# Forgetting attention and a SwiGLU block on one core: q and k read as neighbouring rows, weights spread over later pairs

## The chip, the cores and the metric

The kernel runs on one core of one Trainium2 chip. The metric is the device time of one execution in microseconds. Matrix work runs on TensorE (PE); VectorE (DVE), ScalarE (ACT) and GpSimd (POOL) do the rest, and SyncE (SP) issues most of the transfers between device memory and the on-chip buffer. PE writes its results to PSUM.

## The reference

There are 8 batches of 8 heads, 576 tokens and a head width of 64. The attention result, 4608 tokens by 512, goes through a gated feed-forward block (FFN) with 1536 inner columns.

```python
scores = scale * np.matmul(q, k.transpose(0, 1, 3, 2))
cum = np.cumsum(np.log(np.clip(f, 0.0001, 1.0)), axis=-1)
decay = cum[:, :, :, None] - cum[:, :, None, :]
scores = np.where(causal, -1000000000.0, scores + decay)   # causal: above the diagonal
attn = softmax(scores)                                     # with 1e-09 in the divisor
x = np.matmul(attn, v)                                     # as tokens x (heads * 64)
g = x @ w_gate
out = (g * (1.0 / (1.0 + np.exp(-g))) * (x @ w_val)) @ w_out
```

## The kernel before, in words

**Pairs.** Two heads are worked on together as a pair; there are 32 pairs, four to a batch. For pair `p` the steps are these:

- `load_qk` loads `qf` and `kf` in float32, each with two DMAs (one a head). Partition `r` of 96 holds rows `r`, `r + 96`, and so on, six of them, so each row is a run of 64 numbers, 256 bytes, in memory.
- `cast_qk` makes them `kb` and `qb` in bfloat16. From pair 4 on this runs on POOL alone; before that the planner may also choose ACT or DVE.
- `transposes` (L409) turns `kb` and `qb` on PE into a PSUM tile `tt`, six matmuls of 96 columns each. There is one `tt` buffer. `kt` is copied out by ACT (L415), and the two halves of `qz`, one a head, by DVE or ACT (L420).
- `scores` runs nine blocks of 64 query rows in the order 8, 4, 5, 6, 7, 0, 1, 2, 3. PE writes `sp` (L491, with the mask added by L494); one DVE instruction adds the decay `cb` and takes the minimum, the "reduce" of this text (L507); ACT takes the exponential and its sum (L525). After blocks 8 and 4 to 7, and again after 0 to 3, DVE takes reciprocals `rl` (L534, L535), and POOL writes the normalised blocks into `pk` (L548).
- `turned` transposes `pk` into `pT`: for the first four pairs by PE and copies (L583, L588), later by a DMA transpose from SP (L570). `weighted` multiplies by `v` (L616) and copies into `xT` (L626).

`load_v` brings a batch's `v` in five pieces, `load_cum` the decay of a pair, broadcast over 64 partitions.

**FFN.** There are nine tiles of 512 tokens. A tile needs `xT` of all four pairs of the batches that it touches. For each of 12 column blocks `gate` runs four matmuls each for `gp` and `vp` (L658), then a tanh on ACT (L664) and two DVE instructions (`u` L668, `hh` L674). `project` runs 12 matmuls for each of four output blocks (L705), a copy (L712 or L714) and a store (L718). `gp`, `vp`, `op` and the PSUM tile of `turned` share four PSUM buffers (`gv`).

**Weights.** `weights` loads `wg`, `wv` and `wo` in eleven pieces through POOL's DMA queue (L737, L742), converting to bfloat16 on the way. Each piece waits for a "tick", one particular exponential.

**Order.** Nothing here is in program order. Each step is given to `Planner.add` with the engines it may run on, a due time (`key`), a modelled length and, for DMAs, a modelled time on the transfer queue (`moves`). `Planner.order` plays these forward: each free engine takes the ready step with the lowest key for which buffers are free. The instructions are then emitted in that order on every engine. A change of a modelled length or a key can so move instructions on all five engines. `base(p)` is the due time of a pair, `unit_key(n)` that of an FFN unit:

```python
SLOT0, SLOT = 9.5, 12.0
UNIT = SLOT / 4
def unit_key(n):
    return base(NPB) + 3.0 * SLOT0 + UNIT * n
```

Of the kernel before, what the change touches and what calls it, by code (L numbers as in the profile page):

```python
# [20 lines left out]
class Planner:  # L21
# [4 lines left out]

    LAG = {"PE": 0.25, "DVE": 0.2, "ACT": 0.25, "POOL": 0.12, "SP": 0.0}
    LAND = 2.2

    def __init__(self, counts):  # L30
        self.counts = counts
# [13 lines left out]
    def order(self):  # L45
# [35 lines left out]
        while len(started) < len(steps):  # L81
            moved = True
            while moved:
                moved = False
                for e in self.LAG:
                    if free[e] > t + 1e-9:
                        continue
                    kept, pick = [], None
                    while ready[e]:
                        x = heapq.heappop(ready[e])  # L90
                        n = x[1]
                        if n in started:
                            continue
                        ok = True
                        for b in steps[n][4]:
                            c = b[0]
                            if c in self.counts and len(opened[c]) >= self.counts[c] \
                                    and open_users[opened[c][-self.counts[c]]]:
                                ok = False
                        if ok:  # L100
                            pick = n
                            break
                        kept.append(x)
                    for x in kept:
                        heapq.heappush(ready[e], x)
                    if pick is None:
                        continue
                    n = pick
                    engines, key, fn, needs, opens, moves = steps[n]
                    started.add(n)  # L110
                    for b in opens:
                        if b[0] in self.counts:
                            opened[b[0]].append(b)
                    end = t + engines[e]
                    free[e] = end
                    if moves:
                        queue = max(queue, end) + moves
                        end = queue + self.LAND
                    self.ends[n] = end
                    heapq.heappush(events, (end + self.LAG[e], 0, n))  # L120
                    heapq.heappush(events, (free[e], 1, n))
                    out.append((t, n, e))
                    moved = True
            if not events:
                assert len(started) == len(steps), "the steps wait for each other"
                break
            t = max(t, events[0][0])
            while events and events[0][0] <= t + 1e-9:
# [24 lines left out]
def kernel(  # L153
# [47 lines left out]
            return 0, 1  # L201
        return (g == 1) + c * w, sum(i // 2 >= c for i in GROUPS[g])

    KR, KC = 96, 6
    NRING = 5 * MT
    EARLY = NPB

    consts = ctx.enter_context(tc.tile_pool(name="consts", bufs=1))
    keep = ctx.enter_context(tc.tile_pool(name="keep", bufs=1))
# [58 lines left out]
        return 10.0 + (SLOT0 * p if p <= NPB else SLOT0 * NPB + SLOT * (p - NPB))  # L268

    def unit_key(n):  # L270
        return base(NPB) + 3.0 * SLOT0 + UNIT * n


    def gates():
# [48 lines left out]
        for p in range(2):  # L323
            key = base(0) + 3 if p else -5
            a = add("ACT" if p else "SP", -7 if p else -9, 1.2, load(p), opens=[("t", "fb", p)],
                    moves=0.8)
            a = add("DVE", key, 0.4, clip(("fb", p)), [a], uses=[("t", "fb", p)])
            w = add("ACT", key, 0.6, ln(("fb", p)), [a, w], uses=[("t", "fb", p)])
            ids["cb", p] = add("DVE", key, 1.3, scan(p), [w, o], opens=[("cb", p)],
# [8 lines left out]
    def load_cum(p):  # L338
        def fn():
# [4 lines left out]
                    in_=cum_dram[2 * p + h:2 * p + h + 1, :].to_broadcast((64, S)),  # L344
                )
            st["cb", p] = cb
        ids["cb", p] = add("SP", base(p) - 9, 1.1, fn, [ids["cum"]], opens=[("cb", p)], moves=0.8)

    def zeros():
        def z(n):  # L350
# [15 lines left out]
    def load_qk(p):  # L366
        b, hp = divmod(p, NPB)
        for name, src, off in (("kf", k, -0.2), ("qf", q, 0.0)):
            eng = "ACT" if p == 0 and name == "qf" else "SP"

            def fn(name=name, src=src, eng=eng):
                st[name, p] = ldf.tile([KR, KC, 2, D], F32, name=name)
                for h in range(2):
                    (nc.scalar if eng == "ACT" else nc.sync).dma_start(  # L374
                        out=st[name, p][:, :, h, :],
                        in_=src[b, 2 * hp + h].rearrange("(c r) d -> r c d", r=KR),
                    )

            after = [ids["exp", p - 3, 4]] if p > 2 else [ids["kb", 0]] if p == 2 else []
            ids[name, p] = add(eng, base(p) - 20 + off if p else -8, 1.2, fn, after,  # L380
                               opens=[(name, p)], moves=1.3)

    def cast_qk(p):
        def cq(eng):
            st["qb", p] = att.tile([KR, KC, P], BF16, name="qb")
            qf = st["qf", p].rearrange("r c h d -> r c (h d)")
            if eng is nc.scalar:
                eng.mul(st["qb", p], qf, -scale)
            else:
                eng.tensor_scalar(st["qb", p], qf, -scale, 1.0, op0=ALU.mult, op1=ALU.mult)  # L390

        def ck(eng):
            st["kb", p] = att.tile([KR, KC, P], BF16, name="kb")
            copy_by(nc, eng)(st["kb", p], st["kf", p].rearrange("r c h d -> r c (h d)"))  # L394

        engines = {"POOL": 0.79, "ACT": 0.72, "DVE": 0.88} if p < EARLY else {"POOL": 0.79}
        for name, fn, off in (("kb", ck, -9.2), ("qb", cq, -9)):
# [5 lines left out]
    def transposes(p):  # L403

        def tr(name):
            def fn():
                st["tt", name] = psum([P, S], BF16, "tt", "tt")
                for c in range(KC):
                    nc.tensor.transpose(st["tt", name][:, KR * c:KR * c + KR], st[name, p][:, c, :],  # L409
                                        ident[0:KR, 0:KR])  # L410
            return fn

        def ek(eng):
            st["kt", p] = att.tile([P, S], BF16, name="kt")
            copy_by(nc, eng)(st["kt", p], st["tt", "kb"])  # L415

        def eq(h):
            def fn(eng):
                r = slice(64 * h, 64 * h + 64)
                copy_by(nc, eng)(qzs[p % 2][r, :, h, :],  # L420
                                 st["tt", "qb"][r, :].rearrange("p (i r) -> p i r", r=QB))
            return fn
        a = add("PE", base(p) - 5, 0.3, tr("kb"), [ids["kb", p]], opens=[("tt", p, 0)],
                uses=[("kb", p)])
        ids["kt", p] = [add("ACT", base(p) - 5, 0.54, lambda: ek(nc.scalar), [a], opens=[("kt", p)],
                            uses=[("tt", p, 0)])]
        a = add("PE", base(p) - 4, 0.3, tr("qb"), [ids["qb", p]], opens=[("tt", p, 1)],
                uses=[("qb", p)])
        before = [ids["s", p - 2, i] for i in range(NB)] if p >= 2 else [ids["z", p]]
        ids["qz", p] = [add({"DVE": 0.38, "ACT": 0.53}, base(p) - 4, 0, eq(h), [a] + before,  # L430
                            uses=[("tt", p, 1)]) for h in range(2)]

    def load_v(b):
# [4 lines left out]
        for c in range(5):  # L438
# [17 lines left out]
            buf = ("hh", "v") if b == 0 else ("vf", b, c)  # L456
            opens = [buf] if b or c == 0 else []
            after = [ids["exp", NPB * (b - 1) + min(c, 3), 4] if b else ids["qf", 1]]
            a = add("SP", key, 0.5, load, after, opens=opens, uses=[] if opens else [buf], moves=1.1)
            ids["v", b].append(add({"POOL": 0.58, "ACT": 0.5, "DVE": 0.6} if b == 0 else {"POOL": 0.58},  # L460
                                   key + 10 if b else base(0) + 3 + 0.1 * c, 0,
                                   cast if b == 0 else lambda cast=cast: cast(nc.gpsimd),
# [5 lines left out]
    def scores(p):  # L468
# [8 lines left out]
        for i in ORDER:  # L477
# [6 lines left out]
            for n, (a, z) in enumerate(parts):  # L484
                last = z == L

                def s(i=i, a=a, z=z, last=last):
                    qz = qzs[p % 2].rearrange("p i h r -> p i (h r)")
                    sp = psum([P, 512], F32, "sp", "sp")
                    st["sp", p, i, a] = sp  # L490
                    nc.tensor.matmul(sp[:, :z - a], qz[:, i, :], st["kt", p][:, a:z],  # L491
                                     start=True, stop=not last)
                    if last:
                        nc.tensor.matmul(sp[:, z - a - QB:z - a], ident, mask,  # L494
# [66 lines left out]
    def turned(p, g, n_slots, ns, key):  # L561
# [7 lines left out]
            new()  # L569
            nc.sync.dma_start_transpose(out=st["pT", p, g], in_=src.rearrange("p s k -> p (s k)"))  # L570
        if p >= EARLY:
            m = add("SP", key, 1.35, by_dma, ns, opens=[(f"pT{g}", p)], moves=0.144 * n_slots)
            ids["turn", p, g] = [m]
            ids["pT", p, g] = [m]
            return
# [157 lines left out]
    def weights():  # L733
# [12 lines left out]
        for n in range(4):  # L746
            ids["w", n] = []
            for wt, src in ((wg, moe_w_gate), (wv, moe_w_val)):
                ids["w", n].append(add("POOL", base(0) + 6 + 5 * m, 0.96, piece(wt, src, n),
                                       [ids["tick", m]], moves=2.6))  # L750
                m += 1
        ids["wo"] = []
        for fc in range(0, KF, 4):
            ids["wo"].append(add("POOL", base(0) + 6 + 5 * m, 0.96, piece_out(fc), [ids["tick", m]],
                                 moves=3.4))
            m += 1


# [5 lines left out]
    for b in range(B):  # L764
        for p in range(NPB * b, NPB * b + NPB):
# [4 lines left out]
                load_cum(p)  # L770
            transposes(p)
            scores(p)
            if p == NPB - 1:

                order = [ids["exp", p_, i] for p_ in range(NPB) for i in ORDER]
                for n in range(11):
                    ids["tick", n] = order[2 + 3 * n]
                weights()

            while True:  # L780
                t = ids.get("tiles", 0)
                if t >= NMT or (t + 1) * MT > (b + (p % NPB == NPB - 1)) * S:
                    break
                n = 0 if t == 0 else KF + (t - 1) * (KF + NS)
                for fc in range(KF):
                    gate(t, fc, n)
                    n += 1
                    if t and fc % 3 == 2:
                        project(t - 1, fc // 3, n)
                        n += 1  # L790
                ids["tiles"] = t + 1
        if b + 1 < B:
            load_v(b + 1)
    n = KF + (NMT - 1) * (KF + NS)
    for s_ in range(NS):
        project(NMT - 1, s_, n)
# [34 lines left out]
```

## Time and profile before

| | |
|---|---|
| median of 3 runs | 457.19 us (456.84 to 457.54) |
| the profiled execution's own time | 458.71 us |
| its span, first to last instruction | 456.9 us |
| first FFN matmul starts at | 67.87 us |
| PE busy | 409.9 us (90%), granted clock 0.970 in the mean |
| DVE / ACT / POOL busy | 340.2 / 300.2 / 245.7 us |
| DMA queue q1 (SP) | 213,712 packets, 69.71 MB, 68.4% of 16 engines' span |
| DMA queue q0 (weights) | 5,808 packets, 4.72 MB, 6.8% |

Busy time is what an engine spent in instructions; waits are not in it. The page also cuts the span into 40 slices of 11.4 us and gives each engine's busy tenths in them. A timeline line reads: start in us, length in us, engine, source line, operation, tile written from tile read, size; an idle time before the instruction, with what ended it, stands in brackets. A share of the DMA queues is the time that packets took, summed over queues, so it can pass 100% of 16 engines where packets wait.

### The profile page before, as it was taken

The page shows a single profiled execution, that of the slowest core. Times are in us where ns is not written, and L with a number is a line of the kernel's source. Part 1 is how long each engine was busy: PE and PEld are TensorE (multiplying, and loading weights), DVE is VectorE, ACT ScalarE, POOL GpSimd, SP SyncE. Part 2 cuts the span into 40 slices and gives each one's busy share as a digit, 9 for nine tenths or more (in the row PEclk, how much of TensorE's full clock was granted, in tenths as well). Part 3 has the DMA queues.
Part 4 walks back from the last instruction along what each step waited for, and adds up shares of the span by engine and source line. Part 5 has one row for each costly group of instructions (what it writes and reads, how often), then busy time and mean ns, then how long its engine had stood idle before and what let it go on. Part 6 is the DMA issues. An engine that isn't in the chain of part 4 may idle for free.

```text
span 456.9 us, 9377 instructions
## 1 busy us (share of the span) xinstructions
PE 409.9 (90%) x2788; PEld 211.3 (46%) x2836; DVE 340.2 (74%) x1069; ACT 300.2 (66%) x838; POOL 245.7 (54%) x443
## 2 busy tenths in 40 slices
PE   1557777988989999999999999999999999999996
PEld 0345453444444454554555455445555444444442
DVE  5756578788777989889889888888888864565542
ACT  3875678488776887787887779778777743213210
POOL 5574878378882785666666666666654440000000
PEclk9997589899989999999999999999999999999999
DMA  7999999959997799898799989899983540100103
GB/s 168 181 185 247 213 215 180 220 137 214 227 207 181 133 214 222 179 223 217 190 217 199 207 192 221 192 223 214 196 203 96 99 117 24 46 25 23 46 25 115
DMA packets 220996, 75.77 MB, mean 166 GB/s; under 512 B 206480, under 2 KB 212112, under 8 KB 220944
## 3 DMA queue, kind: packets, MB, share of 16 engines
q1 hardware_dynamic: 213712, 69.71, 68.4%
q0 software_dynamic: 5808, 4.72, 6.8%
q10 hardware_dynamic: 1424, 0.74, 0.7%
q8 instruction: 22, 0.36, 0.3%
q14 instruction: 30, 0.25, 0.2%
HBM read 47.33 MB, written 9.58 MB: 125 GB/s over the span
## 4 chain that ended last, share of the span: by engine, by line
PE 65%; DVE 2%; issue 1%; DMA 1%; ACT 1%; SPq 1%; POOL 0%; DVEq 0%
PE op L705 18%; PE vp L658 17%; PE gp L658 17%; PE sp L491 6%; PE xo L616 5%; PE tt L409 2%; PE sp L494 1%; DMA pT<-pk 1%; DVE t L507 1%; DVE ot L714 0%; DVE rl L534 0%; ACT ev L525 0%; SPq L374 0%; DVE hh L674 0%; POOL pk L548 0%
## 5 line engine op out<-in xcount | busy, mean ns | idle before, releaser
L548 POOL TENSOR_SCALAR pk<-ev,rl 128x512 bf16<-128x512 f32 (+3 forms) x320 | 165.0, 535 | 95.9 <-DVE tm L507 32.7
L525 ACT ACTIVATE ev<-t,tm 128x64 f32<-128x64 f32 (+8 forms) x288 | 159.9, 557 | 40.6 <-DVE tm L507 29.2
L507 DVE CUSTOM_DVE_ANT_0 t<-sp,cb 128x512 f32<-128x512 f32 (+7 forms) x288 | 132.0, 477 | 17.5 <-PE sp L494 9.0
L658 PE MATMUL vp<-xT,wv 128*128 128x512 bf16 x413 | 121.8, 382 | 1.9 <-issue 1.0
L658 PE MATMUL gp<-xT,wg 128*128 128x512 bf16 x418 | 119.1, 385 | 3.8 <-DVE u L668 3.2
L705 PE MATMUL op<-wo,hh 128*128 128x512 bf16 x418 | 119.9, 379 | 0.9 <-DVE u L668 0.2
L491 PE MATMUL sp<-kt,qz 128*128 128x64 bf16 (+1 forms) x319 | 89.7, 298 | 18.5 <-DVE tm L507 15.6
L664 ACT ACTIVATE th<-gp 128x512 f32<-128x512 f32 x108 | 62.5, 588 | 58.2 <-PE gp L658 57.0
L668 DVE SCALAR_TENSOR_TENSOR u<-th,gp 128x512 f32<-128x512 f32 x108 | 73.2, 684 | 33.4 <-ACT th L664 33.1
L674 DVE TENSOR_TENSOR hh<-u,vp 128x512 bf16<-128x512 f32 x108 | 73.3, 682 | 15.0 <-PE vp L658 12.8
L705 PEld LDWEIGHTS <-hh 128*128 128x128 bf16 x432 | 39.2, 98 | 42.9 <-issue 0.8
L494 PE MATMUL sp<-mask,ident 128*128 128x64 bf16 x288 | 55.7, 198 | 0.0
L525 ACT ACTIVATION_READ_ACCUMULATOR ev<-t,tm 128x1 f32 x288 | 54.6, 190 | 0.0
L658 PEld LDWEIGHTS <-wg 128*128 128x128 bf16 x432 | 36.4, 99 | 37.0 <-issue 6.2
L658 PEld LDWEIGHTS <-wv 128*128 128x128 bf16 x432 | 36.1, 98 | 34.1 <-issue 1.4
L491 PEld LDWEIGHTS <-qz 128*128 128x128 bf16 x320 | 32.0, 101 | 39.0 <-issue 5.5
L494 PEld LDWEIGHTS <-ident 128*128 128x128 bf16 x288 | 28.5, 99 | 36.7 <-issue 17.5
L616 PE MATMUL xo<-pT,vt 128*64 128x320 bf16 (+4 forms) x448 | 35.5, 274 | 3.6 <-ACT vt L454 1.9
L616 PEld LDWEIGHTS <-vt 128*64 128x64 bf16 x448 | 20.4, 110 | 26.4 <-issue 17.0
L626 ACT CAST xT<-xo 128x320 bf16<-128x320 f32 x64 | 25.0, 390 | 11.0 <-PE xo L616 10.6
L394 POOL CAST kb<-kf 96x768 bf16<-96x768 f32 x30 | 27.0, 900 | 7.2 <-DMA kf<-in_k_dram 7.2
L454 POOL CAST vt<-vf 128x512 bf16<-128x512 f32 (+1 forms) x35 | 21.4, 610 | 17.4 <-DMA vf<-in_v_dram 12.1
(50 smaller groups left out, 283.0 us busy)
## 6 DMA issues: line engine op xcount, KB each, us to landing
kf<-in_k_dram SPq DMA_DIRECT2D x64, 144.0 KB, 3.3
out_dram<-ot SPq DMA_DIRECT2D x36, 256.0 KB, 2.6
qf<-in_q_dram SPq DMA_DIRECT2D x62, 144.0 KB, 3.5
cb<-cum_f SPq DMA_DIRECT2D x60, 144.0 KB, 3.4
vf<-in_v_dram SPq DMA_DIRECT2D x28, 256.0 KB, 3.6
wg<-in_moe_w_gate_dram POOLq DMA_DIRECT2D x4, 384.0 KB, 7.3
wv<-in_moe_w_val_dram POOLq DMA_DIRECT2D x4, 384.0 KB, 9.2
wo<-in_moe_w_out_dram POOLq DMA_DIRECT2D x3, 512.0 KB, 10.2
```

The source lines that it names most:

```text
L394: copy_by(nc, eng)(st["kb", p], st["kf", p].rearrange("r c h d -> r c (h d)"))
L491: nc.tensor.matmul(sp[:, :z - a], qz[:, i, :], st["kt", p][:, a:z], start=True, stop=not last)
L494: nc.tensor.matmul(sp[:, z - a - QB:z - a], ident, mask, start=False, stop=True)
L507: nc.vector.tensor_tensor_reduce(out=st["t", p, i][:, a:z], in0=st["sp", p, i, a][:, :z - a], in1=st["cb", p][:, a:z], scale=1.0, scalar=init,
L525: nc.scalar.activation(evs[i][:, :L], st["t", p, i][:, :L], AF.Exp, bias=tm[:, i:i + 1], scale=-1.0, accum_out=ls[:, i:i + 1])
L548: nc.gpsimd.tensor_scalar(pks[p % 2][:, s0:s0 + w * (m - 1) + 1:w, :], evs[i][:, P * c:P * (c + m)].rearrange("p (c k) -> p c k", k=P), st ...
L616: nc.tensor.matmul(xo[64 * h:64 * h + 64, 0:n * QB], vt[:, c, 2 * hp + h, :], pT[:, s0:s0 + n, h, :], start=(c == 0), stop=(c == nch - 1))
L658: nc.tensor.matmul(st[name, t, fc], w_[:, ko, fc * P:(fc + 1) * P], xT[:, ko, x0:x0 + MT], start=(ko == 0), stop=(ko == KD - 1))
L664: nc.scalar.activation(st["th", t, fc], st["gp", t, fc], AF.Tanh, scale=0.5)
L668: nc.vector.scalar_tensor_tensor(st["u", t, fc], st["th", t, fc], 1.0, st["gp", t, fc], op0=ALU.add, op1=ALU.mult)
L674: nc.vector.tensor_mul(st["hh", t][:, fc, :], st["u", t, fc], st["vp", t, fc])
L705: nc.tensor.matmul(st["op", t, s_], st["hh", t][:, fc, s_ * P:(s_ + 1) * P], wo[:, fc, :], start=(fc == 0), stop=(fc == KF - 1))
```

## The change

Six things are edited.

1. `q` and `k` are read so that a partition holds neighbouring rows: six for `k` (96 partitions, runs of 1536 bytes), eight for `q` (72 partitions, runs of 2048 bytes). Both heads come in one DMA. The tile is laid out head first; the cast puts chunks first again.
2. `k` is transposed in six matmuls of 96 columns as before, `q` in eight of 72. A transposed chunk now holds every sixth or eighth token, and the copies out of PSUM put them in order: they read PSUM with a step of 96 or 72 elements.
3. The weights' ticks go from exponentials 2, 5, ... 32 of the first four pairs to 9, 13, ... 49, which is pairs 1 to 5.
4. Pair 0's `k` and `q` get an earlier key than the loads of `f`, so that they lead the queues of SP and ACT.
5. The planner gets a limit: a step that opens a buffer and moves data is held back while the modelled transfer queue is more than 5 us long. FFN units are due one `SLOT0` (9.5) later. Some modelled lengths and `moves` change.
6. The FFN tiles and the weights are added to the plan after a batch's pairs, from batch 1 on, instead of after each pair. Their dependencies are the same.

```diff
+    CHUNKS = {"k": (96, 6), "q": (72, 8)}
+    WFIRST, WSTEP = 9, 4
 # Planner
+    AHEAD = 5.0
+                        if steps[n][5] and queue - t > self.AHEAD:
+                            heapq.heappush(events, (queue - self.AHEAD, 2, n))
+                            ok = False
 # unit_key
-        return base(NPB) + 3.0 * SLOT0 + UNIT * n
+        return base(NPB) + 4.0 * SLOT0 + UNIT * n
 # load_qk
-                st[name, p] = ldf.tile([KR, KC, 2, D], F32, name=name)
-                for h in range(2):
-                    (nc.scalar if eng == "ACT" else nc.sync).dma_start(
-                        out=st[name, p][:, :, h, :],
-                        in_=src[b, 2 * hp + h].rearrange("(c r) d -> r c d", r=KR),
-                    )
+                nr, nch = CHUNKS[name[0]]
+                st[name, p] = ldf.tile([nr, 2, nch, D], F32, name=name)
+                (nc.scalar if eng == "ACT" else nc.sync).dma_start(
+                    out=st[name, p].rearrange("r h c d -> r h (c d)"),
+                    in_=src[b, 2 * hp:2 * hp + 2].rearrange("h (r c) d -> r h (c d)", c=nch),
+                )
...
-            ids[name, p] = add(eng, base(p) - 20 + off if p else -8, 1.2, fn, after,
-                               opens=[(name, p)], moves=1.3)
+            ids[name, p] = add(eng, base(p) - 20 + off if p else -10, 0.6, fn, after,
+                               opens=[(name, p)], moves=1.0)
 # cast_qk (kb likewise)
-            st["qb", p] = att.tile([KR, KC, P], BF16, name="qb")
-            qf = st["qf", p].rearrange("r c h d -> r c (h d)")
+            st["qb", p] = att.tile([*CHUNKS["q"], 2, D], BF16, name="qb")
+            qf = st["qf", p].rearrange("r h c d -> r c h d")
 # transposes
-                for c in range(KC):
-                    nc.tensor.transpose(st["tt", name][:, KR * c:KR * c + KR], st[name, p][:, c, :],
-                                        ident[0:KR, 0:KR])
+                nr, nch = CHUNKS[name[0]]
+                for c in range(nch):
+                    nc.tensor.transpose(st["tt", name][:, nr * c:nr * c + nr],
+                                        st[name, p][:, c, :, :].rearrange("r h d -> r (h d)"),
+                                        ident[0:nr, 0:nr])
...
-            copy_by(nc, eng)(st["kt", p], st["tt", "kb"])
+            nr, nch = CHUNKS["k"]
+            copy_by(nc, eng)(st["kt", p].rearrange("p (r c) -> p r c", c=nch),
+                             st["tt", "kb"].rearrange("p (c r) -> p r c", c=nch))
...
-                copy_by(nc, eng)(qzs[p % 2][r, :, h, :],
-                                 st["tt", "qb"][r, :].rearrange("p (i r) -> p i r", r=QB))
+                nr, nch = CHUNKS["q"]
+                copy_by(nc, eng)(
+                    qzs[p % 2][r, :, h, :].rearrange("p i (r c) -> p i r c", c=nch),
+                    st["tt", "qb"][r, :].rearrange("p (c i r) -> p i r c", c=nch, i=NB))
...
-        ids["qz", p] = [add({"DVE": 0.38, "ACT": 0.53}, base(p) - 4, 0, eq(h), [a] + before,
+        ids["qz", p] = [add({"DVE": 0.6, "ACT": 0.55}, base(p) - 4, 0, eq(h), [a] + before,
 # the ticks of the weights
-                order = [ids["exp", p_, i] for p_ in range(NPB) for i in ORDER]
+            order = [ids["exp", p, i] for p in range(2 * NPB) for i in ORDER]
...
-                    ids["tick", n] = order[2 + 3 * n]
+                ids["tick", n] = order[WFIRST + WSTEP * n]
```

More of the change, by code (lines that the diff above doesn't have):

```diff
@@ L202, in slots_of @@
         return (g == 1) + c * w, sum(i // 2 >= c for i in GROUPS[g])
-    KR, KC = 96, 6
+    CHUNKS = {"k": (96, 6), "q": (72, 8)}
     NRING = 5 * MT
     EARLY = NPB
+    WFIRST, WSTEP = 9, 4
     consts = ctx.enter_context(tc.tile_pool(name="consts", bufs=1))
@@ L325, in gates @@
             a = add("ACT" if p else "SP", -7 if p else -9, 1.2, load(p), opens=[("t", "fb", p)],
-                    moves=0.8)
+                    moves=1.0)
             a = add("DVE", key, 0.4, clip(("fb", p)), [a], uses=[("t", "fb", p)])
@@ L346, in fn @@
             st["cb", p] = cb
-        ids["cb", p] = add("SP", base(p) - 9, 1.1, fn, [ids["cum"]], opens=[("cb", p)], moves=0.8)
+        ids["cb", p] = add("SP", base(p) - 9, 1.1, fn, [ids["cum"]], opens=[("cb", p)], moves=1.0)
     def zeros():
@@ L392, in ck @@
         def ck(eng):
-            st["kb", p] = att.tile([KR, KC, P], BF16, name="kb")
-            copy_by(nc, eng)(st["kb", p], st["kf", p].rearrange("r c h d -> r c (h d)"))
+            st["kb", p] = att.tile([*CHUNKS["k"], 2, D], BF16, name="kb")
+            copy_by(nc, eng)(st["kb", p], st["kf", p].rearrange("r h c d -> r c h d"))
         engines = {"POOL": 0.79, "ACT": 0.72, "DVE": 0.88} if p < EARLY else {"POOL": 0.79}
@@ L424, in transposes @@
                 uses=[("kb", p)])
-        ids["kt", p] = [add("ACT", base(p) - 5, 0.54, lambda: ek(nc.scalar), [a], opens=[("kt", p)],
+        ids["kt", p] = [add("ACT", base(p) - 5, 0.56, lambda: ek(nc.scalar), [a], opens=[("kt", p)],
                             uses=[("tt", p, 0)])]
@@ L458, in load_v @@
             after = [ids["exp", NPB * (b - 1) + min(c, 3), 4] if b else ids["qf", 1]]
-            a = add("SP", key, 0.5, load, after, opens=opens, uses=[] if opens else [buf], moves=1.1)
+            a = add("SP", key, 0.5, load, after, opens=opens, uses=[] if opens else [buf], moves=1.45)
             ids["v", b].append(add({"POOL": 0.58, "ACT": 0.5, "DVE": 0.6} if b == 0 else {"POOL": 0.58},
@@ L490, in s @@
                     st["sp", p, i, a] = sp
-                    nc.tensor.matmul(sp[:, :z - a], qz[:, i, :], st["kt", p][:, a:z],
+                    nc.tensor.matmul(sp[:, :z - a], qz[:, i, :],
+                                     st["kt", p][:, a:z],
                                      start=True, stop=not last)
@@ L571, in turned @@
         if p >= EARLY:
-            m = add("SP", key, 1.35, by_dma, ns, opens=[(f"pT{g}", p)], moves=0.144 * n_slots)
+            m = add("SP", key, 1.35, by_dma, ns, opens=[(f"pT{g}", p)], moves=0.16 * n_slots)
             ids["turn", p, g] = [m]
@@ L749, in weights @@
                 ids["w", n].append(add("POOL", base(0) + 6 + 5 * m, 0.96, piece(wt, src, n),
-                                       [ids["tick", m]], moves=2.6))
+                                       [ids["tick", m]], moves=2.8))
                 m += 1
@@ L754, in weights @@
             ids["wo"].append(add("POOL", base(0) + 6 + 5 * m, 0.96, piece_out(fc), [ids["tick", m]],
-                                 moves=3.4))
+                                 moves=3.1))
             m += 1
@@ L772 @@
             scores(p)
-            if p == NPB - 1:
-                order = [ids["exp", p_, i] for p_ in range(NPB) for i in ORDER]
-                for n in range(11):
-                    ids["tick", n] = order[2 + 3 * n]
[L778 to L791, printed above, removed]
         if b + 1 < B:
             load_v(b + 1)
+        if b == 1:
+            order = [ids["exp", p, i] for p in range(2 * NPB) for i in ORDER]
+            for n in range(11):
+                ids["tick", n] = order[WFIRST + WSTEP * n]
+            weights()
+        while b:
+            t = ids.get("tiles", 0)
+            if t >= NMT or (t + 1) * MT > (b if b + 1 < B else B) * S:
+                break
+            n = 0 if t == 0 else KF + (t - 1) * (KF + NS)
+            for fc in range(KF):
+                gate(t, fc, n)
+                n += 1
+                if t and fc % 3 == 2:
+                    project(t - 1, fc // 3, n)
+                    n += 1
+            ids["tiles"] = t + 1
     n = KF + (NMT - 1) * (KF + NS)
```

## The prediction

> **What bounds the kernel now.** I read the page's busy shares first, then its slices, then the windows of 5 and 25 us, and last the timelines of the first 90 us. The page, parts 1 and 2:
>
> ```profile
> PE 409.9 (90%) x2788; PEld 211.3 (46%) x2836; DVE 340.2 (74%) x1069; ACT 300.2 (66%) x838; POOL 245.7 (54%) x443
> PE   1557777988989999999999999999999999999996
> DMA  7999999959997799898799989899983540100103
> ```
>
> PE is 47 us short of the span. The slices (11.4 us each) say where: among the first twelve are 1, 5s, 7s and 8s, after that all are 9 but the end. From 150 to 450 us the windows leave 4.4 us idle of 300. So a gain must come from the first 135 us, or from fewer PE nanoseconds later. The first FFN matmul stands at 67.87 us; call that F. Up to 68 us PE is idle 29 us (39.05 busy), from there to 135 us another 9.8.
>
> Why is F so late? The DMA view for 0 to 68 us, then timelines of SP, POOL, DVE and PE (start, length, what it is, idle before it):
>
> ```profile
> q1 hardware_dynamic: 26102, 8.15, 55.1%
> q0 software_dynamic: 5808, 4.72, 45.7%
> ```
> ```profile
> 17.34 9.61 SPq L448 DMA_DIRECT2D hh<-in_v_dram  x4
> 27.04 2.12 SPq L374 DMA_DIRECT2D qf<-in_q_dram  x2
> ...
> 78.79 1.00 SPq L374 DMA_DIRECT2D qf<-in_q_dram  x2
> ```
> ```profile
> 46.10 0.82 POOL L390 TENSOR_SCALAR qb<-qf 96x768 bf16<-96x768 f32 x1 [2.79 <-DMA qf<-in_q_dram]
> 46.89 0.80 POOL L737 DMA_DIRECT2D wg<-in_moe_w_gate_dram  x1
> ```
> ```profile
> 39.45 0.68 DVE L507 CUSTOM_DVE_ANT_0 t<-sp,cb 128x512 f32<-128x512 f32 x1
> ...
> 46.82 0.69 DVE L507 CUSTOM_DVE_ANT_0 t<-sp,cb 128x512 f32<-128x512 f32 x1 [0.22 <-ACT kt L415]
> ...
> 58.55 0.69 DVE L507 CUSTOM_DVE_ANT_0 t<-sp,cb 128x512 f32<-128x512 f32 x1 [0.22 <-ACT ev L525]
> ```
> ```profile
> 52.02 2.85 PE L583 MATMUL pt<-ident,pk 128*128 128x128 bf16 x25 [1.81 <-POOL pk L548]
> ```
>
> The two queues together take over 100% of 16 engines: weights (q0) and 256-byte rows (q1) fill them. SP needs 9.61 us for four v issues, against about 0.5 us each when uncongested; the q load of pair 2 goes out behind them at 27.04 and is cast at 35.03 on DVE. The q of pair 3 holds POOL for 2.79 us, two weight issues follow, and so the normalised blocks reach PE at 52.02.
>
> The first reduce of pairs 0 to 5 stands at 12.46, 21.82, 39.45, 46.82, 58.55 and 68.52 us. The last interval, 9.97 us, is the only late one with no DMA wait and no weight issue in it. Its chain is reciprocal (57.75), POOL normalise, PE transposes (61.70), copies, weighted sum, the next exps, reciprocal (67.0): 9.25 us.
>
> **The change, part by part.**
>
> *Longer rows.* In 0 to 68 us, 30 k and q transfers of 576 packets run on q1: 17,280 packets. One costs 0.551 x 68 x 16 / 26,102 us = 23.0 ns, so together 397 us over 16 engines, 24.8 us of all of them. The same 15 tensors are 4.42 MB. The bounds for the new rows: 2 KB stores in 400 to 425 us move 32 GB/s at a share of 0.09, so 355 GB/s, which makes 12.5 us; the weights' packets (1.5 or 2 KB read, cast on the way) cost 0.457 x 1088 / 5808 us = 85.6 ns, and 2,544 of these make 13.6 us. I take 13: 12 us of DMA are saved before F, about 1.6 us a pair later. Later they are worth nothing, since PE is full. SP's issues for k and q fall from four a pair to two, and the planner's new AHEAD, which keeps a load back while its modelled queue is over 5 us long, only orders SP's list: about 0.5 us an issue, on an engine that waits anyway.
>
> The trace has no transfer over 72 partitions. The Trainium skill, DMA: Bandwidth & Descriptors, "Why a DMA increments its semaphore by 16 and not by 1", says that a copy spreads over the largest number up to 16 that divides both outer dims: 16 for 96 rows, only 12 for 72. By it q would take 1.11 us instead of 0.83, still far under its 1.65 now, and the sum would stand.
>
> *Weights later.* All eleven pieces are issued between 15.9 and 56 us and cost 31 us of 16 engines. Spread over pairs 1 to 5 the three wo pieces (1.57 of 4.72 MB, 10 us) go past F. Demand before F falls from 72 us to about 50, in some 62 us of time: the queues are no longer full, and the waits above go. What is late next is the 9.97 us chain. The later wo is covered: in the built order its first user comes after pair 8's scores have begun, and the last piece is tied to pair 5.
>
> *F.* With every interval at 9.97, pair 5's first reduce comes at 12.46 + 49.85 = 62.3 instead of 68.5, 6.2 us sooner. Against it: weight issues (0.75 to 0.80 us) stand between the normalise instructions of pairs 1 and 2 (+1.5), and the copies (below) add 0.6. F therefore moves by -4.1; the bounds are -8 (9.25 us a pair, nothing added) and 0.
>
> *k and q first in their queues.* In the built order PE has the k transposes of pairs 0 and 1 ahead of the first scores, and DVE both scans ahead of the first reduce. With one PSUM buffer for `tt`, pair 0's scores now queue behind pair 1's k: its load, its cast on DVE, and pair 0's `kt` copy. The first load lands sooner, the second wait is new: +1.5 to -1.5; I take 0.
>
> *Copies out of PSUM.* ACT `kt` is 632 ns, `qz` 450 (DVE) and 633 (ACT). No row reads PSUM with a step. Lower bound: no change. Upper: twice, +1.2 us on ACT and +0.45 on DVE a pair. In 150 to 350 us DVE is busy 21.4 of 25 us and ACT 20, two pairs a window: 1.7 us and 2.3 us of slack a pair cover even that. Before F nothing covers it. I take +0.25 on DVE only: at the rate of its 128x512 float reduce (0.69 us) 576 elements take 0.7 to 0.8 us, and ACT's 633 ns show no such faster rate to lose. That is on the chain (`qz` stands ahead of the reciprocal at 66.26), but half of it lies beside DVE's own waits of 0.2 to 0.4 us: 0.6 in five pairs. POOL's `qb` cast goes from 768 to 1,024 columns, 0.83 to 1.1 us, covered by the 2.0 us that POOL waits before the next blocks at 67.20.
>
> *Two more q transposes a pair.* 52 matmuls after F. These rows of PE give the price:
>
> ```profile
> 74.08 0.42 PE L409 MATMUL tt<-ident,kb 96*128 96x96 bf16 x6
> 74.34 0.19 PE L491 MATMUL sp<-kt,qz 128*128 128x64 bf16 x1
> 74.37 0.19 PE L494 MATMUL sp<-mask,ident 128*128 128x64 bf16 x1
> ```
>
> Six transposes, each with its weight load, take 0.26 us from start to next start: 43 ns each for 96 columns; the 64-column matmul takes 30. Eight of 72 columns hold the same 576 columns: 0 to +86 ns a pair, over 26 pairs 0 to 2.3 us. I take +0.6, nearer the column price.
>
> Here a rule speaks against the change. The Trainium skill, TensorE: Matmul & The Clock Gate, "LDWEIGHTS (loading the stationary operand)", prices a load by its columns alone, 107 ns for 128; unhidden, the 52 would cost 5.6 us and nearly eat the gain. The trace disagrees: load records last 95 to 101 ns, yet load and matmul together repeat every 43 ns.
>
> *The order after F.* Before, PE runs 28 gate matmuls against 7 of scores at 74 to 85 us and stops:
>
> ```profile
> 80.56 3.31 PE L658 MATMUL gp<-xT,wg 128*128 128x512 bf16 x8 [3.19 <-DVE u L668]
> ```
>
> The wait is 3.19 us, and the eight after it start 389 ns apart (granted clock 0.66 in that window) against 215 later: 1.4 us more. In the built order the gates are even, 32, 58 and 84 by the ends of pairs 6, 7 and 8 (before: 26, 62, 80). I count two thirds of 4.6: -3. Bounds 0 and -7: by the end of pair 10 the new order has issued 32 more FFN matmuls, 6.9 us at 216 ns. FFN starts some 0.3 pair earlier in the attention order, so PE owes 0.4 more later.
>
> **Sum:** -4.1 + 0 + 0.6 - 3 + 0.4 = -6.1. The profiled execution took 458.71 us (span 456.9), 1.52 above the median of the runs, so 452.6 for its like and 451.1 for the median.
>
> **Rivals.**
> 1. *The chain hides the relief.* Pairs are already tied to 9 to 10 us by POOL, and the weight issues move into the normalise blocks, so F stays; the order brings the -3 or less, PE pays 1 to 2. 455 to 458. For: POOL is busy 44.65 of the first 68 us. Against: 39.45 - 21.82 = 17.6 us is no chain.
> 2. *Stepped copies.* They double: before F +1.6 us in each of five pairs on ACT and DVE, +8, and DVE, busy 4.97 of 5 us in several windows up to 110 us, gives +2 more. -6.1 - 0.6 + 10 makes +3.3, 460.5, slower. It decides from about +1 us a pair. For: no contiguous row can exclude it. Against: ACT, at 632 ns for 576 elements, shows no packed rate to lose.
> 3. *A new stall in the order.* Two like that at 80.56, 4.6 us each, at other places: 460.
> 4. *Everything comes out:* F -8, order -7, and 1 us of costs: 443.
>
> **How the numbers follow.** Forecast 0.52 (own range 445 to 456), rival 1 0.13, rival 2 0.13, rival 3 0.10, rival 4 0.12. About 0.2% (0.9 us) is what a measurement can tell here. Faster: 0.52 + 0.12 + half of rival 1 + a little of rival 2 = 0.72; same 0.06, mostly rival 1; slower 0.22. The range, 441.5 to 460, takes rival 4 at its low end and rivals 2 and 3 about to their values.
>
> **What would show it.** Right: the first 68 us no longer over 100% of the queues, SP issues near 0.5 us; pair intervals near 10 us, F at 62 to 65; six and eight transposes alike at about 0.26 us; no PE wait of 3 us behind `u`. Wrong: F at 67 or later with quiet queues (rival 1); `kt` or `qz` above 1 us (rival 2); PE holes after F (rival 3); q transposes near 0.8 us.

## The result and the profile after

| | before | after |
|---|---|---|
| median of four runs beside each other | 457.01 us (456.49 to 457.54) | 451.88 us (451.03 to 452.3) |
| profiled execution, its span | 458.71, 456.9 | 451.03, 449.3 |
| F, the first FFN matmul | 67.87 | 61.23 |
| from F to the end of the span | 389.0 | 388.1 |
| mean granted clock | 0.970 | 0.984 |

The ratio is 0.9885 [0.9867, 0.9904], faster by 5.1 us. Ratios, here and below, leave out executions in a slow state (one of e2's twelve, two of e11's twelve), medians do not. The page after, parts 1 and 2 (the granted clock is the last line):

```profile
PE 406.9 (91%) x2850; PEld 209.1 (47%) x2900; DVE 346.6 (77%) x1071; ACT 302.2 (67%) x838; POOL 247.1 (55%) x441
PE   1577798998799999999999999999999999999996
DMA  8998979999999999999988789988882520101003
PEclk9998889999899999999999999999999999999999
```

The 9s of PE begin a slice or two earlier; slice 11 is now a 7. Busy PE time fell although there are 64 more transposes; the mean granted clock rose. The DMA view, 0 to 68 us:

```profile
q1 hardware_dynamic: 14372, 9.26, 55.8%
q0 software_dynamic: 4080, 3.05, 33.2%
```

q1 sends 14,372 packets where it sent 26,102, and they take the same share: the new packets cost more each. The two queues fell from 101 to 89%, all of it q0's, whose last three pieces (`wo`) now go out behind F, at 70.9 to 77.6 us. SP's issues, then DVE's first reduces of pairs 2, 3 and 4:

```profile
7.63 8.09 SPq L463 DMA_DIRECT2D hh<-in_v_dram  x5
...
24.04 0.52 SPq L381 DMA_DIRECT2D kf<-in_k_dram  x1
24.66 0.46 SPq L381 DMA_DIRECT2D qf<-in_q_dram  x1
```
```profile
33.12 0.69 DVE L523 CUSTOM_DVE_ANT_0 t<-sp,cb 128x512 f32<-128x512 f32 x1 [0.22 <-ACT ev L541]
...
42.82 0.69 DVE L523 CUSTOM_DVE_ANT_0 t<-sp,cb 128x512 f32<-128x512 f32 x1 [0.22 <-ACT ev L541]
...
52.71 0.69 DVE L523 CUSTOM_DVE_ANT_0 t<-sp,cb 128x512 f32<-128x512 f32 x1 [0.22 <-ACT ev L541]
```

Five `v` issues still hold SP for 8.09 us, but early; a `k` or `q` issue takes 0.5. The first reduces of pairs 0 to 5 are at 14.83, 22.63, 33.12, 42.82, 52.71 and 62.28: the late intervals are 9.6 to 9.9, and the 17.6 us one is gone. The start is 2.4 us later than before. PE around F and at the eight `q` transposes, and the copies out of PSUM (groups by form):

```profile
61.23 0.38 PE L674 MATMUL gp<-xT,wg 128*128 128x512 bf16 x1 [0.16 <-issue]
...
73.11 0.42 PE L417 MATMUL tt<-ident,qb 72*128 72x72 bf16 x8
73.37 0.60 PE L674 MATMUL vp<-xT,wv 128*128 128x512 bf16 x2
```
```profile
L434 DVE COPY qz<-tt 64x576 bf16<-64x576 bf16 x33 | 24.7, 750 | 3.9 <-PE tt L417 2.1 <-ACT qz L434 1.6
L426 ACT COPY kt<-tt 128x576 bf16<-128x576 bf16 x32 | 20.2, 630 | 3.4 <-PE tt L417 3.4
L434 ACT COPY qz<-tt 64x576 bf16<-64x576 bf16 x31 | 19.6, 631 | 12.9 <-DVE qz L434 11.5 <-PE tt L417 1.2
```

Eight transposes take 0.26 us, as six did. The step costs DVE 0.30 us a copy (450 to 750 ns) and ACT nothing.

### The profile page after: what moved, and what is told of

Its sections match the earlier page's. It is cut to its first block, busy times and chain, and to the rows that moved or that the text cites. A ratio compares the mean times of both kernels' runs of the same rounds, so it can differ in the third digit from the quotient of the medians.

```text
span 449.3 us, 9390 instructions
## 1 busy us (share of the span) xinstructions
PE 406.9 (91%) x2850; PEld 209.1 (47%) x2900; DVE 346.6 (77%) x1071; ACT 302.2 (67%) x838; POOL 247.1 (55%) x441
## 4 chain that ended last, share of the span: by engine, by line
PE 58%; DVE 6%; ACT 4%; issue 2%; DMA 0%; another core or an unknown queue 0%; DVEq 0%; ACTq 0%
PE op L721 17%; PE gp L674 15%; PE vp L674 14%; PE sp L506 6%; PE xo L632 4%; ACT ev L541 2%; DVE t L523 2%; PE tt L417 2%; DVE qz L434 1%; PE sp L510 1%; ACT th L680 1%; DVE ot L730 1%; DVE u L684 1%; ACT qz L434 1%; DVE hh L690 0%
## 5 line engine op out<-in xcount | busy, mean ns | idle before, releaser
L541 ACT ACTIVATE ev<-t,tm 128x576 f32<-128x576 f32 (+8 forms) x288 | 159.7, 556 | 25.9 <-DVE tm L523 19.0
L506 PE MATMUL sp<-kt,qz 128*128 128x512 bf16 (+4 forms) x320 | 88.9, 298 | 17.9 <-DVE tm L523 13.8
L680 ACT ACTIVATE th<-gp 128x512 f32<-128x512 f32 x108 | 63.6, 591 | 57.7 <-PE gp L674 56.8
L510 PE MATMUL sp<-mask,ident 128*128 128x64 bf16 x288 | 55.6, 197 | 0.0
L721 PEld LDWEIGHTS <-hh 128*128 128x128 bf16 x432 | 37.2, 98 | 38.3 <-issue 0.8
L632 PE MATMUL xo<-pT,vt 128*64 128x320 bf16 (+4 forms) x448 | 34.6, 271 | 1.2 <-ACT xT L642 1.0
L730 DVE TENSOR_SCALAR ot<-op 128x512 f32<-128x512 f32 x27 | 18.6, 689 | 19.7 <-PE op L721 18.1
L642 ACT CAST xT<-xo 128x320 bf16<-128x320 f32 x64 | 24.9, 389 | 11.3 <-PE xo L632 11.1
L401 POOL CAST kb<-kf 96x768 bf16<-96x768 f32 x30 | 25.0, 835 | 11.8 <-ACT qb L395 9.6
```

Source lines behind the costliest of these rows:

```text
L401: copy_by(nc, eng)(st["kb", p], st["kf", p].rearrange("r h c d -> r c h d"))
L510: nc.tensor.matmul(sp[:, z - a - QB:z - a], ident, mask, start=False, stop=True)
L541: nc.scalar.activation(evs[i][:, :L], st["t", p, i][:, :L], AF.Exp, bias=tm[:, i:i + 1], scale=-1.0, accum_out=ls[:, i:i + 1])
L632: nc.tensor.matmul(xo[64 * h:64 * h + 64, 0:n * QB], vt[:, c, 2 * hp + h, :], pT[:, s0:s0 + n, h, :], start=(c == 0), stop=(c == nch - 1))
L680: nc.scalar.activation(st["th", t, fc], st["gp", t, fc], AF.Tanh, scale=0.5)
L721: nc.tensor.matmul(st["op", t, s_], st["hh", t][:, fc, s_ * P:(s_ + 1) * P], wo[:, fc, :], start=(fc == 0), stop=(fc == KF - 1))
```

## The experiments

The first four ask whether the longer rows and the later weights made the gain, as the prediction said. All edits are to the kernel after unless another is named. The texts on record name their theories themselves.

**Old rows, all else as after (e1).** The planner's numbers are kept, so the engines keep their order.

```diff
-    CHUNKS = {"k": (96, 6), "q": (72, 8)}
+    CHUNKS = {"k": (96, 6), "q": (96, 6)}
-                    out=st[name, p].rearrange("r h c d -> r h (c d)"),
-                    in_=src[b, 2 * hp:2 * hp + 2].rearrange("h (r c) d -> r h (c d)", c=nch),
+                    out=st[name, p],
+                    in_=src[b, 2 * hp:2 * hp + 2].rearrange("h (c r) d -> r h c d", c=nch),
 # and the copies out of PSUM plain, as before
```

> The changed kernel with the old row layout of q and k: 256-byte runs, six chunks of 96 rows for both, plain copies out of PSUM; one DMA a tensor, every other instruction and its place as in the changed kernel. Theory A (the longer rows free the queues before the first FFN matmul, F): F goes from 61.2 back to about 64, DMA issues of several us return on SP, time 454 to 455. Rival B (the longer rows free nothing: in the changed kernel q1 still takes 59.7% of 16 engines up to 62 us with 14,212 packets, against 55.1% with 26,102 before): F within 0.7 us of 61.2, time 451 to 452, a little lower for the cheaper copies (DVE qz back from 0.75 to 0.45 us).

Measured: 452.0 us (448.35 to 453.98), ratio 0.9867 [0.9826, 0.9907]. F is 58.95, 2.3 us earlier than after, where neither theory had it fall. The profiled execution, at 449.8, loses 1.0 of this again behind F; it is 2.2 below the median, and of a slower execution there is no profile. With the weights late, the longer rows bring nothing that can be measured.

**Early weights, all else as after (e2).**

```diff
-    WFIRST, WSTEP = 9, 4
+    WFIRST, WSTEP = 2, 3
```

> The changed kernel with the weights' ticks back at exponentials 2, 5, ... 32. Theory A and rival B: the queues are over-full again in pairs 0 to 3, pair intervals of 11 us and more, F at 64 to 67, time 454 to 457. Rival C (what F gained came from the new order of the steps, not from transfers): F within 1 us of 61.2, time 451 to 453.

Measured: 455.86 us (454.06 to 460.9), 0.9961 [0.9939, 0.9983]; F 65.45, as theories A and B had it. With the long rows, the late ticks are worth 3.5 us by the ratios. This edit does not bring back the weights of before: point 6 of the change stays, and the three `wo` pieces are still issued behind F, at 72.3 to 82.0 us, where before had them at 53.5 to 55.6. The same holds for e3 (66.6 to 76.6).

**Both of these undone (e3).** 

> Both undone: old rows and early weights, in the changed kernel's planner settings. Theory A: the two losses add, F about 67, time 457 to 458. Rival B: like the early weights alone, 454 to 457. Rival C: 451 to 453.

Measured: 447.99 us (446.83 to 450.54), 0.9797 [0.9764, 0.9831]; F 59.64, the first reduces at 14.10, 21.77, 31.54, 41.27 and 51.16. That is below all three theories: with the old rows and the early ticks the kernel is faster than with the new ones, by 0.9%. And its queues are as full as before's. The DMA view of e3, 0 to 62 us:

```profile
q1 hardware_dynamic: 27908, 8.70, 63.4%
q0 software_dynamic: 3963, 2.96, 35.9%
q10 hardware_dynamic: 1408, 0.74, 5.0%
```

That is 104% of 16 engines (before's three queues, counted alike over 68 us, take 105%), with single SP issues of up to 4.6 us, and still no gap of 17 us. So full queues alone do not make that gap.

**The loads alone (e4).** One execution, four stages on SP's queue, 16 tensors of 288 KB each: two DMAs a tensor of 256-byte rows as before; runs of 1536 bytes on 96 partitions; runs of 2048 on 72; 256-byte rows in one DMA.

> Loads alone, nothing of the computation: 16 tensors of 288 KB (k and q of eight pairs) in each of four stages, one after the other: 256-byte rows in two DMAs a tensor; 96 partitions with 1536-byte runs; 72 partitions with 2048-byte runs; 256-byte rows in one DMA a tensor. Theory A (step 'longer rows'): 26 us for the first and last stage, 13 us for the second and third. Rival B: all stages alike within 15%. The rule on 12 of 16 engines for 72 partitions: the third stage takes 4/3 of the second.

Windows of e4, one from within each stage (us, length, DVE, POOL, PE's clock, DMA share, GB/s):

```profile
9.00:12.00 3.00, 0.62 (x4) 0.00 (x0) 1.00 1.38 202
...
36.00:39.00 3.00, 0.93 (x6) 0.00 (x0) 1.00 1.10 261
...
54.00:57.00 3.00, 0.83 (x6) 0.00 (x0) 1.00 0.79 213
...
81.00:84.00 3.00, 0.62 (x4) 0.00 (x0) 1.00 1.37 201
```

A tensor takes 1.45, 1.13, 1.37 and 1.45 us. The pair's two loads thus go from 2.9 to 2.5 us: 0.4 saved. Neither theory fits. A queue that does nothing but short rows reads 1.38, so before's 1.01, a mean over 68 us, does not show a full queue (its windows of 8 to 10 us between 30 and 68 us read 1.15 to 1.22), and a share does not turn into bandwidth across packet sizes.

**Which part of the long rows costs at early weights?** e5 is e2 with `q` in the old rows and plain copies, `k` long; e6 is e2 with `q`'s copies plain and all else long; it leaves out the sorting of `q`'s rows. The edit of e6:

```diff
-                    qzs[p % 2][r, :, h, :].rearrange("p i (r c) -> p i r c", c=nch),
-                    st["tt", "qb"][r, :].rearrange("p (c i r) -> p i r c", c=nch, i=NB))
+                copy_by(nc, eng)(qzs[p % 2][r, :, h, :],
+                                 st["tt", "qb"][r, :].rearrange("p (i r) -> p i r", r=QB))
```

> The kernel of e2_early (455.9 us) with q alone back in the old layout (256-byte rows, six chunks of 96, plain copies); k keeps its 1536-byte runs. Same place of every instruction. Theory Q (q's part is what costs: 72 partitions, a cast of 1,024 columns, DVE's copy of 0.75 us): it comes near e3_both, 448 to 450 us, F near 59.6. Theory K (the cost lies in the loads of both, or in k's copy): half way or less, 452 to 456.

> The kernel of e2_early with q's copies out of PSUM made plain; this leaves out the sorting of q's rows, so its output is another. Loads, casts and eight transposes stay. If DVE's 0.3 us a pair is what q's part costs, F falls by 1.5 to 3 us and the time to 450 to 453. If loads and casts are the cost, 454 to 456.

Measured: e5 447.65 us, 0.9773 [0.9739, 0.9807], F 59.04; e6 450.94 us, 0.9829 [0.9799, 0.986], F 63.47. By the ratios `q`'s new form costs e2 1.9% (8.6 us), of which the stepped copy is 1.3% (6.0 us); `k`'s long rows cost nothing. With late weights the whole of it costs nothing that can be measured (e1 against after); why the weights decide this stays open.

**The other planner numbers.** e7 is e3 with FFN due as before, e8 is e3 without the limit of 5 us on queued transfers.

```diff
-        return base(NPB) + 4.0 * SLOT0 + UNIT * n
+        return base(NPB) + 3.0 * SLOT0 + UNIT * n
 # e8
-    AHEAD = 5.0
+    AHEAD = 1.0e9
```

> The kernel of e3_both (old rows, early weights, the new planner settings: 448.0 us) with the FFN's due time back from 4 to 3 SLOT0. Theory P1 (a later due time keeps the FFN out of the first pairs and evens its pace): time up by 3 to 6 us. Theory P2 (the lead of k and q and the AHEAD limit made the gain): within 1.5 us of 448.

> The kernel of e3_both without the AHEAD limit (set to 1e9). Theory P2: SP issues run into a full queue again (issues of several us), F back to 64 or more, time 452 to 456. Theory P1: within 1.5 us of 448.

Measured: 447.76 us, 0.9779 [0.9749, 0.981], and 447.6 us, 0.9754 [0.9729, 0.9779]. Neither number makes the gain.

**One number in the kernel before (e9).** What then? In before, pair 2's scores stand late in the order written for PE. PE's timeline of before (`xo` is the weighted sum of pair 0, `pt` the transposes of pair 1's probabilities, `sp` at 39.16 the first score of pair 2):

```profile
31.73 0.60 PE L616 MATMUL xo<-pT,vt 128*64 128x320 bf16 x6
34.27 0.37 PE L616 MATMUL xo<-pT,vt 128*64 128x192 bf16 x2 [1.94 <-ACT vt L454]
34.96 0.26 PE L616 MATMUL xo<-pT,vt 128*64 128x64 bf16 x2 [0.32 <-DVE vt L454]
36.16 1.57 PE L583 MATMUL pt<-ident,pk 128*128 128x128 bf16 x13 [0.94 <-POOL pk L548]
...
39.16 0.26 PE L491 MATMUL sp<-kt,qz 128*128 128x64 bf16 x1 [0.22 <-issue]
```

Pair 2's `kt` had been copied by 21.6 and its `qz` by 23.6 us (the copy of `kt` at 32.15 is pair 3's). The scores stood behind work that waited for `vt` and `pk`, and on DVE the first reduce stood behind the copies of `pt`. But this reduce also reads the pair's decay `cb`. DVE waits for its two transfers, the first two of these four issues of SP, as the last thing before that reduce:

```profile
29.21 2.95 SPq L342 DMA_DIRECT2D cb<-cum_f  x4
```

They went out behind the `v` and `q` issues of 17.34 and 27.04 and landed 6.6 and 6.9 us after they were issued, the second at 36.70. The reduce came at 39.45. So the written order of PE and DVE alone accounts for its last 2.8 us; until 36.70 the decay would have held it too. e9 gives pair 0's loads the earlier key of the change, and nothing else; the planner then writes another order:

```diff
-            ids[name, p] = add(eng, base(p) - 20 + off if p else -8, 1.2, fn, after,
+            ids[name, p] = add(eng, base(p) - 20 + off if p else -10, 1.2, fn, after,
```

> The kernel before with one number changed: the key of pair 0's loads is -10 where it was -8, so that k and q lead their queues. Rows, moves, lengths and weights are before's. In the written order pair 2's scores then stand ahead of pair 1's transposes of probabilities, where before had them behind pair 0's weighted sum. Theory O (the order that the planner writes is what brings the first FFN matmul forward): 448 to 453 us at a before of 457, first FFN matmul at 60 to 63 us, first reduces of pairs 1 to 4 about 10 us apart with no gap of 17. Rival (the gain needs the single issue, the lengths given to the planner, or the limit on queued transfers): 456 to 458, first FFN matmul at 66 to 69.

Measured: 449.6 us (449.11 to 450.37) against 456.73 beside it, ratio 0.9844 [0.9821, 0.9868]. F is 63.46 (expected 60 to 63), the gap between pairs 1 and 2 11.1 us. PE's timeline of e9, pair 2's scores now ahead of pair 1's transposes, then its decay and its queues up to F:

```profile
34.32 0.41 PE L491 MATMUL sp<-kt,qz 128*128 128x512 bf16 x2
...
37.86 2.21 PE L583 MATMUL pt<-ident,pk 128*128 128x128 bf16 x19
```
```profile
24.92 2.38 SPq L342 DMA_DIRECT2D cb<-cum_f  x4
```
```profile
q1 hardware_dynamic: 25415, 7.76, 57.0%
q0 software_dynamic: 5656, 4.58, 48.0%
q10 hardware_dynamic: 1424, 0.74, 4.8%
```

The decay of pair 2 has landed at 28.65, 8 us earlier, and the reduce comes at 35.80. So the one number moved the decay on SP as well as the scores on PE, and the run does not divide the gain between them. The queues take 110%, with all eleven weight pieces issued before F: fuller queues than before's, and F 4.4 us earlier. One due time, with the rows, issues, weights and lengths of before, brings at least what the whole change does, by the order that the planner then writes.

**One DMA a tensor in before (e10).** Short rows, the same order on every engine.

```diff
 # the tile is laid out head first, and the casts and transposes read it so
-                for h in range(2):
-                    (nc.scalar if eng == "ACT" else nc.sync).dma_start(
-                        out=st[name, p][:, :, h, :],
-                        in_=src[b, 2 * hp + h].rearrange("(c r) d -> r c d", r=KR),
-                    )
+                (nc.scalar if eng == "ACT" else nc.sync).dma_start(
+                    out=st[name, p],
+                    in_=src[b, 2 * hp:2 * hp + 2].rearrange("h (c r) d -> r h c d", r=KR),
+                )
```

> The kernel before with one transfer for each of q's and k's tensors in place of one for each head (the packets stay 256 bytes, and every engine's order is that of before). Theory O: nothing, 456 to 458 us, first FFN matmul at 67 to 69, the gap of 17 us between the first reduces of pairs 1 and 2 still there. Rival (the issues on the sync engine held the loads): 450 to 454, first FFN matmul at 62 to 65.

Measured: 454.71 us, 0.997 [0.9945, 0.9994]; F 65.74, the gap still 16.9 us. Fewer issues are worth some 1.4 us, where nothing was expected. The decay lands at 34.35 here, 2.4 us earlier than in before, and pair 2's first reduce still comes 3.5 us behind it, at 37.85: an earlier decay alone does not close the gap in that order.

**The lead taken out again (e11 of after, e12 of e3).** The key is -8 in both.

> The kernel after with the key of pair 0's loads back at -8: forget gates ahead of k and q. Pair 2's scores still stand ahead of pair 1's transposes in the order that comes out. Theory O (it is the order that counts, not the lead in itself): 450 to 453 us at a before of 457, the first reduce of pair 0 about 2 us earlier than the 14.8 of the kernel after, first FFN matmul at 59 to 62. Rival (the lead in itself brings the gain): 455 to 458, first FFN matmul at 65 to 68.

> The kernel with old rows and early weights of e3, and the key of pair 0's loads back at -8. The order that comes out has pair 0's whole weighted sum ahead of pair 2's scores and pair 1's transposes behind these: between that of before and that of e3. Theory O: 447 to 452 us at a before of 457, first FFN matmul at 59 to 63. Rival (the lead in itself): 455 to 458, first FFN matmul at 65 to 68.

Measured: e11 455.19 us, 0.9958 [0.9931, 0.9985], first reduce at 13.14, F 60.23; e12 452.27 us, 0.9898 [0.9876, 0.9921], F 62.90. e12, just above what theory O had, has neither the lead nor the new rows nor the late ticks, and is still 1.0% faster than before: what is left of the change is the single issue, the planner's other numbers with the order that they write, and the `wo` pieces behind F. In e11 F came out as expected and the time did not: 393.7 us lie behind F, 5.6 more than after. PE and POOL of e11:

```profile
101.50 0.43 PE L417 MATMUL tt<-ident,kb 96*128 96x96 bf16 x6 [1.85 <-POOL kb L401]
108.82 1.01 PE L721 MATMUL op<-wo,hh 128*128 128x512 bf16 x2 [6.89 <-DMA wo<-in_moe_w_out_dram]
```
```profile
94.03 2.04 POOL L564 TENSOR_SCALAR pk<-ev,rl 128x512 bf16<-128x512 f32 x4
96.02 0.80 POOL L758 DMA_DIRECT2D wo<-in_moe_w_out_dram  x1
```

In that order the last `wo` piece is issued at 96.02, behind POOL's normalising, and lands 12.8 us later; PE stands for 6.89 us until then. After has it issued at 77.59 and never waits for it. The later weights thus leave a price open that the order may or may not call in. With the lead all three families are faster: by 1.6% in before, 0.7% in after, 1.0% in e3. In after this is not F's doing: F is 60.23 without the lead and 61.23 with it.

## Why the prediction was right, point by point

The time (451.1 against 451.88) and the sign came out. Several steps did not, so the closeness is in part luck: the forecast moved by -6.1, the medians by -5.1 and the two profiled spans by -7.6.

- *F, -4.1.* Measured -6.6. Intervals of 9.97 us came (9.6 to 9.9 for the late ones), but not for the reason given. "The queues are no longer full, and the waits above go" is the step that failed: e3 has queues at 104% and F at 59.64, e9 queues at 110% and F at 63.46. The `q` load at 27.04, cast at 35.03, is pair 3's, not pair 2's as I read it (so 46.10 is pair 4's). What went out behind the long `v` issues for pair 2 was its decay, there at 36.70; from then to 39.45 the written order of PE and DVE held the first reduce. I had read the waits of POOL and SP, and neither what stands ahead of pair 2's scores on PE nor the third input of the reduce. A due time that changes the orders of SP and PE together took the gap to 11.1 us (e9).
- *Longer rows, "about 1.6 us a pair".* Mis-sized: 0.4 us (e4). The 355 GB/s came from stores, and queue time by packet is no throughput. Nothing reached the time.
- *Weights later.* The late ticks are worth 3.5 us with the new rows (e2), nothing of the kind with the old (e3 is 0.7% faster than e1, with intervals that just overlap). That the `wo` pieces go behind F was undone in no run of the changed kernel, and is not priced by itself. "The later wo is covered" held in after, but only by its order: e11 pays 6.89 us.
- *The lead, 0 within 1.5.* The start was delayed by 2.4 us, 1.7 of it by the lead (e11: 13.14), beyond the bound. The number that makes the lead was worth -7.1 us in before (e9), through the order it causes, and about -3.3 in after (e11), all of it behind F. The prediction looked at its effect on pair 0 alone and had it at nothing.
- *Copies.* DVE's 0.7 to 0.8 was right (0.750), ACT unchanged was right. Of its price of 0.6 nothing is seen with late ticks; with early ones the stepped copy costs about 6.0 (e6). Rival 2's mechanism exists, then, without ACT's half of it.
- *Two more transposes.* 0.26 us for eight: the lower bound, nothing, where 0.6 was taken. The rule of the Trainium skill, TensorE: Matmul & The Clock Gate, "LDWEIGHTS (loading the stationary operand)", a price by columns alone, would put eight loads of 128 columns at 0.86 us by estimate, if none of it were hidden. In the trace the eight loads and their matmuls together take 0.26.
- *Twelve of sixteen engines.* Of the rule in the Trainium skill, DMA: Bandwidth & Descriptors, "Why a DMA increments its semaphore by 16 and not by 1", e4 shows the share: 0.79 for 72 partitions beside 1.10 for 96, a ratio of 0.72 to the rule's 0.75. The time of a tensor rises only 1.21-fold, not 1.33.
- *After F, -3 + 0.6 + 0.4.* Measured -1.0. The 3.19 us wait behind `u` is gone (0.4 in all now), but smaller holes of the kind of rival 3 opened elsewhere, at 110 to 125 us:

```profile
111.89 0.24 PE L506 MATMUL sp<-kt,qz 128*128 128x192 bf16 x1 [1.54 <-DVE tm L523]
...
124.05 0.42 PE L506 MATMUL sp<-kt,qz 128*128 128x512 bf16 x2 [1.42 <-ACT qz L434]
```

So F gave 2.5 more than predicted and the rest 1.0 less; the sum was near because the errors stood against each other. Rival 1 (F stays) and rival 4 (443) are out. Left open: how e9's gain splits, since 4.4 of its 8.3 us of span lie before F and 3.9 behind, in an order that differs on every engine. A kernel with only pair 2's scores moved, or only its decay, was not tried, and what the modelled lengths and point 6 do by themselves was not either.

The fastest versions are those with `q` in the old rows and the early ticks: e3, e5, e7 and e8, at ratios of 0.975 to 0.980, all faster than after.

## What to carry to other kernels

Where a planner writes the order, a changed due time or modelled length is a change of the kernel in its own right: run it alone, before the memory layout that it came with gets the credit. When a step starts late on an in-order engine, list what stands ahead of it there, and every input it reads with the time when it landed, before blaming one load. Cost a new transfer shape by a run of that shape alone; shares of the queues do not compare across packet sizes.

## What the runs showed of the hardware

- A full queue of 256-byte rows reads a share of 1.37 to 1.38 at 201 to 203 GB/s; runs of 1536 bytes on 96 partitions reach 261, only 1.29 times as much for rows six times as long. One DMA or two for a tensor is the same, 1.45 us.
- DVE loses 300 ns on 64x576 bfloat16 from PSUM when it reads with a step; ACT loses nothing.
- The granted clock reads lower before than after in the same stretch of time, but the profiles do not show by what rule. Windows of before, after and e9 (PE, PEld, DVE, ACT, POOL, clock, DMA share, GB/s):

```profile
50.00:60.00 10.00, 6.53 (x54) 4.67 (x53) 5.69 (x22) 5.75 (x19) 8.42 (x16) 0.64 1.22 219
```
```profile
50.00:60.00 10.00, 7.91 (x84) 5.35 (x81) 7.32 (x32) 8.64 (x25) 8.94 (x16) 0.83 0.90 202
```
```profile
37.00:41.00 4.00, 4.00 (x35) 3.22 (x36) 3.00 (x9) 3.47 (x9) 4.00 (x7) 0.57 1.24 232
```

In the first two the clock is lower where PE has more holes; in the third PE has none, and the clock is lower still. In it 19 transposes (37.86) took 2.21 us; the same 19 at 46.43, where 46 to 48 us read 1.00, took 1.24. Part of the gain before F may so be clock and not idle time. How much was not taken apart.
